# Attention and routed MoE on one core: logits and row transposes of two pairs of chunks together, other gating groups, constants beside chunk 0

## The chip, the cores and the metric

One core of one Trainium2 chip runs the whole program. The metric is the time of one execution on the device in microseconds, the median of several runs. TensorE is called PE here, VectorE DVE, ScalarE ACT, GpSimd POOL and SyncE SP; SP issues most DMAs.

## The reference, cut to what matters

Four batches of 768 tokens, eight heads of 64 dimensions. A decayed linear attention gives `x` of 3072 tokens by 512 features; a gate picks one of eight experts for each token, and that expert's two matrices (512 to 1024 to 512) are applied.

```python
for t in range(S):
    state = gamma * state + einsum('bhd,bhe->bhde', k[:, :, t], v[:, :, t])
    y[:, :, t] = scale * einsum('bhd,bhde->bhe', q[:, :, t], state)
x = y.transpose(0, 2, 1, 3).reshape(B * S, H * D)
logits = x @ w_gate
expert_idx = argmax(logits, axis=1)
gate_w = softmax(logits)[arange(N), expert_idx]
out[mask_e] = gate_w * (relu(x[mask_e] @ w1[e]) @ w2[e])      # for each expert e
```

All in float32; large products of the experts are split into a high and a low part.

## The kernel before, in words

The tokens are cut into 24 chunks of 128 (`C`), six to a batch (`CPB`). Twelve periods (`for n in range(last + 1)`, L545) each finish a pair of chunks, a = 2n and b = 2n + 1. The order in each engine's queue is written out by hand (`manual_schedule`): what stands first in the code stands first on its engine, and each engine works its queue in that order.

In a period PE does, in this order: `carry(n)` (the state's part of both outputs, L281), then the visit to the pair before: `logits(n - 1)` (L347), `rows` twice (transposes of `xT` into rows, L316) and `finish_logits` (transposes of the logits back to tokens, L356); then `update(b)` (L264, not at a batch's last chunk), `output(a)` and `output(b)` (L298), the `rank` products of a group where one is chosen (L408), `update(a + 2)`, and the scores of the next two chunks (L251). Four banks of PSUM, tags s0 to s3, hold the scores of two chunks, and between them the row transposes (s0 and s1).

ACT copies logits to `LT` (L353), transposed rows to `xrow` (L324), the state to `ub` (L275) and expert 0's weights to their high part (L139). DVE masks the scores (`Sb`, L260), evicts the outputs to `xT` (L312), reduces logits and does the gating. POOL scales v (`scale`, L238), makes the decay powers (`grow`), cuts low parts of weights (L140), and sends rows: `scatter_rows` (L758) writes one chunk's 128 rows of x to DRAM at the places that `KEY` names, by an indirect DMA.

Gating goes by groups of chunks, `GROUPS` (L44, first chunk and count): a group is chosen in the period after its last pair (`chosen`, L541): argmax, ranks within the expert, places, weights, and the label beside each row. Then its rows may be sent. Which chunks are sent where stands in three tables: `BEHIND` (L46, at the end of period n, behind the eviction of its second chunk), `AMID` (L47, behind the copy `LT` of period n) and `AFTER` (L48, behind the state's copy of `update(a + 2)`). Each entry has two chunks, and a small POOL copy to `gated` (L331) ahead of them waits for the named tile. Chunks 16 and 17 are sent in period 9 (`soon`, L590) as soon as they are labelled, and the first 320 rows of expert 0 are then fetched (`fetch_early`), turned in period 11 (`turn_early`) and used by the first expert's products, which fill PE's queue from there on (`early_pieces`, L801, first bank s2).

`xrow` holds a batch's six chunks, in two buffers. Chunks come by `load` (L223) on SP's queue, halves first: q and k turned (part 0), v and k as they are (part 1). `SPLITS` (L55) says in which period pieces of expert 0's weights are cut, `fetches` (L540) when the third quarter of them is fetched. Before the first chunk PE runs `WARM` products of ones (L506). Constants `cst` come in two DMAs, one on ACT's queue (L494) and one on SP's (L501).

The steps of the period that the change touches, as they stand in the loop:

```python
if n in AMID:
    send_behind(state["LT"][:, 0:1], AMID[n])
rows(a - 2, "s0")
rows(a - 1, "s1")
finish_logits(n - 1)
...
if n in BEHIND:
    send_behind(xTs[n][:, 0, C:C + 1], BEHIND[n])
...
    update(a + 2)
if n in AFTER:
    send_behind(ubs[(a + 2) % 3][:, 0, 0:1], AFTER[n])
...
    scale(a + 4)
```

Behind period 11 come the last pair's logits and rows, groups 4 and 5, the tail of the first expert's products and then the loop over the other experts.

Of the kernel before, what the change touches and what calls it, by code (L numbers as in the profile page):

```python
# [9 lines left out]
F32 = mybir.dt.float32  # L10
# [28 lines left out]
SLICE = P + 2  # L39
ROW = 4 * SLICE  # L40
MAXB = CMAX32 // 32
WARM = 10
FILL = (1, 3, 4)
GROUPS = ((0, 6), (6, 6), (12, 4), (16, 2), (18, 4), (22, 2))  # L44
FULL = 18
BEHIND = {3: (0, 1), 4: (4, 5), 6: (6, 7), 7: (10, 11), 8: (12, 13)}  # L46
AMID = {4: (2, 3), 7: (8, 9)}  # L47
AFTER = {8: (14, 15)}  # L48
AHEAD = 4
FIRST = AHEAD + 11  # L50
MID = (19, 20)
LATER = {6: (15, 16), 7: (17,), 8: (18,), 9: (19,), 10: (20,)}
_PIECES = {2: 3, 3: 2, 5: 3, 6: 1, 7: 3}
_ORDER = iter([(part, i) for part in range(4) for i in range(4)])
SPLITS = {n: tuple(next(_ORDER) for _ in range(c)) for n, c in _PIECES.items()}  # L55
BIG = 1 << 20
# [9 lines left out]
NCONST = _n  # L66
NFIRST = OFF["iota"][0]
NLOAD = OFF["ahead"][0]


def _constants():
# [30 lines left out]
def retention_moe(ctx, tc, qkv, w1, w2, cst, out):  # L102
# [102 lines left out]
    with ExitStack() as actx:  # L205
# [32 lines left out]
        def scale(g, engine=nc.gpsimd):  # L238
            c = g % CPB
            vs = wk.tile([P, H, D], F32, name="vs", bufs=3)  # L240
            engine.tensor_tensor(
                out=vs, in0=qs[g][:, 2].rearrange("a (h d) -> a h d", d=D),
                in1=cv[:, c, :].unsqueeze(2).broadcast_to([P, H, D]), op=ALU.mult)
# [63 lines left out]
        def evict(g):  # L307
            Y, c = Ys[g // 2], g % CPB
            if g % 2 == 0:
                xTs[g // 2] = wk.tile([P, NP, TW], F32, name="xT")  # L310
            xT = xTs[g // 2][:, :, (g % 2) * C:(g % 2 + 1) * C]
            nc.vector.tensor_tensor(out=xT.rearrange("a (r m) t -> a r m t", m=2), op=ALU.mult,  # L312
                                    in0=Y[:, :, 2 * (g % 2) * C:2 * (g % 2 + 1) * C].rearrange("a r (m t) -> a r m t", m=2),
                                    in1=G[:, c].rearrange("a (r m) t -> a r m t", m=2))

        def rows(g, tag, ps=ps_s):  # L316
# [7 lines left out]
            nc.scalar.copy(out=xrows[b][:, c, :, 0:P].rearrange("t q (k r) -> t q k r", r=32),  # L324
                           in_=tr.rearrange("t k (q r) -> t q k r", r=32))

        gated = gsm.tile([P, 1], F32, name="gated")
# [5 lines left out]
                send_rows(g)  # L333

        def send_rows(g):
            b, c = divmod(g, CPB)
            sent = scatter_rows(tc, x_rows, KEY[:, g, 0:1], xrows[b][:, c].rearrange("t q m -> t (q m)"), "sorted")

        def pad_rows(which, count, first):
            nc.vector.tensor_scalar(out=pads[:, which], in0=count, scalar1=k_("pos")[:, 0:1], scalar2=first,  # L340
# [4 lines left out]
            return scatter_rows(tc, x_rows, pads[:, i:i + 1], cs[:, 0:ROW], "sorted")  # L345

        def logits(t):  # L347
            L = bank(0, "L", (P, TW)) if t == NCH // 2 - 1 else ps_1.tile([P, TW], F32, name="L", tag="misc")
            for p in range(NP):
                nc.tensor.matmul(out=L[32 * p:32 * p + 32, :], lhsT=wgs[:, p, :], rhs=xTs[t][:, p, :],  # L350
                                 start=True, stop=True)
            LT = wk.tile([P, TW], F32, name="LT", bufs=1)
            nc.scalar.copy(out=LT, in_=L)  # L353
            state["LT"] = LT

        def finish_logits(t):  # L356
            i = [n for n, (a, w) in enumerate(GROUPS) if a <= 2 * t < a + w][0]
            a, w = GROUPS[i]
            both = ps_1.tile([P, 2, TW], F32, name="lp", tag="misc")
            lp, state["spare"] = both[:, 0].rearrange("p (c n e) -> p c n e", c=2, n=NP), both[:, 1]  # L360
            for ci in range(2):
                nc.tensor.transpose(out=lp[:, ci].rearrange("t p e -> t (p e)"),
                                    in_=state["LT"][:, ci * C:(ci + 1) * C], identity=ident)
            if w == 2:
                lgs[i] = state["spare"][:, 3 * w * E:4 * w * E].rearrange("p (i e) -> p i e", e=E)
            elif 2 * t == a:
                lgs[i] = gsm.tile([P, w, E], F32, name=f"lg{w}")
            nc.vector.tensor_reduce(out=lgs[i][:, 2 * t - a:2 * t - a + 2, :], axis=AX.X, op=ALU.add,
                                    in_=lp[:, :, :, 0:E].rearrange("t c p e -> t c e p"))


        exs = gsm.tile([P, CPB, E + 1], F32, name="exs")
# [1 line left out]
        def gating(i):  # L374
# [10 lines left out]

            def choose():

                lg, eq, pr = [state["spare"][:, n * w * E:(n + 1) * w * E].rearrange("p (i e) -> p i e", e=E)
                              for n in range(3)]
                mx, ed = v["mx"], v["ed"] = sm("mx"), sm("ed")  # L390
                nc.vector.tensor_reduce(out=mx, in_=lgs[i], axis=AX.X, op=ALU.max)  # L391
                if w == 2:
# [46 lines left out]
                nc.vector.reciprocal(out=gw, in_=gw)  # L439

            def label():
                b, c = divmod(a, CPB)
                x = xrows[b][:, c:c + w]
# [101 lines left out]
        for n in range(last + 1):  # L545
# [8 lines left out]
            if n > 0:  # L554
                if n == last:
                    turn_early()
                if n != soon:
                    logits(n - 1)
                if n == last:
                    for j, w, _ in first["pieces"]:  # L560
                        cut_high(nc, first["x"][0], first["xt"], j, w)
                if n in AMID:
                    send_behind(state["LT"][:, 0:1], AMID[n])
                rows(a - 2, "s0")
                rows(a - 1, "s1")
                finish_logits(n - 1)
            if n == 7:
                for i in SPLITS[n]:
# [653 lines left out]
```

## Time and profile before

| | |
|---|---|
| median of 3 runs | 413.22 us (411.82 to 414.07) |
| profiled execution, its own time | 408.67 us |
| its span, first to last instruction | 406.8 us |
| PE busy | 391.1 us (96%) |
| DVE, ACT, POOL busy | 239.9, 140.4, 181.5 us |
| mean granted clock of PE | 0.994 |
| DMA | 81.57 MB, 201 GB/s over the span |

The profiled execution is one run; its span leaves out what lies around the first and the last instruction. In a line of a timeline the first number is the start in us from the span's beginning, the second how long the merged instructions took together; in brackets stands how long the engine was idle ahead of it and what ended that.

### The profile page before, as it was taken

To read this page: it belongs to the slowest core of one execution; us is meant where nothing else is said; L and a number is where in the kernel's file an instruction comes from. 1 tells how busy PE (TensorE), PEld (TensorE's weight loads), DVE (VectorE), ACT (ScalarE), POOL (GpSimd) and SP (SyncE) were. 2 spreads that over 40 slices of the span, in tenths; PEclk is the share of its full clock that TensorE was granted. 3 is DMA by queue.
4 is the path that set the end of the run, shared out by engine and by line. 5 is a ranking of instruction groups with operands and counts; after the bars stand their busy time and mean duration, and the time that the engine had idled before them with its cause. 6 is when DMAs were issued, how large, how long until landed. Compare 5 with 4: busy or idle time off the path is not lost. (4 is left out here: it accounts for less than half of the span.)

```text
span 406.8 us, 8297 instructions
## 1 busy us (share of the span) xinstructions
PE 391.1 (96%) x3273; PEld 360.8 (89%) x3273; DVE 239.9 (59%) x468; ACT 140.4 (35%) x247; POOL 181.5 (45%) x176
## 2 busy tenths in 40 slices
PE   8999899889988999999999999999999999999985
PEld 5887787768888989999999999999999999999864
DVE  3467457756653478583847475667737748656111
ACT  1233244222521455531533343244334325424000
POOL 3647856562170507400374067028407714832722
PEclk9999999999999999999999999999999999999989
DMA  8999999937047939655543746284655546610101
GB/s 286 415 406 408 414 417 411 382 151 198 1 183 158 357 106 231 247 205 109 205 148 124 188 160 234 46 232 166 178 143 189 195 97 216 196 70 15 52 33 46
DMA packets 42328, 81.57 MB, mean 201 GB/s; under 512 B 4458, under 2 KB 18158, under 8 KB 39856
## 3 DMA queue, kind: packets, MB, share of 16 engines
q1 hardware_dynamic: 36768, 67.44, 49.5%
q0 software_dynamic: 5376, 13.49, 8.9%
q8 instruction: 26, 0.43, 0.4%
q10 hardware_dynamic: 144, 0.09, 0.2%
q14 instruction: 14, 0.11, 0.1%
HBM read 65.93 MB, written 15.68 MB: 201 GB/s over the span
## 5 line engine op out<-in xcount | busy, mean ns | idle before, releaser
L759 POOL DMA_INDIRECT out<-Z,sidx x90 | 102.8, 1142 | 142.5 <-DVE Z L940 117.2
L140 DVE TENSOR_TENSOR wlo<-raw,whi 128x1024 fp32r<-128x1024 f32 (+1 forms) x61 | 69.8, 1154 | 14.9 <-ACT whi L139 9.3
L139 ACT CAST whi<-raw 128x1024 fp32r<-128x1024 f32 (+1 forms) x72 | 67.1, 950 | 6.2 <-DMA raw<-w 6.1
L1083 PE MATMUL py<-hh,whi 128*128 128x452 f32 (+5 forms) x192 | 67.0, 349 | 0.0
L1083 PE MATMUL py<-hl,whi 128*128 128x452 f32 (+5 forms) x192 | 67.0, 349 | 0.0
L1083 PE MATMUL py<-hh,wlo 128*128 128x452 f32 (+5 forms) x192 | 66.8, 348 | 0.0
L1060 ACT ACTIVATE hh<-ph 128x452 fp32r<-128x452 f32 (+6 forms) x56 | 28.2, 506 | 88.6 <-PE ph L1055 71.2
L1061 DVE SCALAR_TENSOR_TENSOR hl<-ph,hh 128x452 fp32r<-128x452 f32 (+6 forms) x56 | 32.0, 574 | 39.3 <-ACT hh L1060 34.6
L1055 PE MATMUL ph<-xh,wlo 128*128 128x452 f32 (+6 forms) x224 | 50.1, 345 | 0.0
L1055 PE MATMUL ph<-xh,whi 128*128 128x452 f32 (+6 forms) x224 | 50.1, 345 | 0.0
L1055 PE MATMUL ph<-xl,whi 128*128 128x452 f32 (+6 forms) x224 | 50.0, 345 | 0.0
L1055 PEld LDWEIGHTS ph<-xh,whi 128*128 128x128 f32 x224 | 40.8, 188 | 0.9
L1055 PEld LDWEIGHTS ph<-xh,wlo 128*128 128x128 f32 x224 | 40.7, 188 | 0.8
L1055 PEld LDWEIGHTS ph<-xl,whi 128*128 128x128 f32 x224 | 40.7, 188 | 0.7
L1083 PEld LDWEIGHTS py<-hl,whi 128*128 128x128 f32 x192 | 36.0, 188 | 1.1 <-issue 0.3
L1083 PEld LDWEIGHTS py<-hh,whi 128*128 128x128 f32 x192 | 36.0, 188 | 1.0 <-ACT hh L1060 0.3
L1083 PEld LDWEIGHTS py<-hh,wlo 128*128 128x128 f32 x192 | 36.1, 188 | 0.7
L759 POOL DMA_INDIRECT x_sorted<-xrow,KEY x24 | 25.2, 1049 | 18.2 <-DVE mx L391 8.1
L781 ACT CAST xh<-buf 128x512 fp32r<-128x512 f32 (+7 forms) x26 | 14.3, 556 | 54.4 <-DVE buf L774 45.2
L260 DVE TENSOR_TENSOR Sb<-sp,cs 128x512 f32<-128x512 f32 x48 | 29.9, 682 | 4.4 <-PE sp L257 4.4
L935 DVE STREAM_TRANSPOSE Z<-py 128x416 f32<-128x416 f32 (+3 forms) x24 | 15.0, 625 | 21.3 <-PE py L1083 18.2
L304 PE MATMUL Y<-Sb,vs 128*64 128x128 f32 x384 | 24.6, 275 | 1.4 <-issue 1.4
(173 smaller groups left out, 535.7 us busy)
## 6 DMA issues: line engine op xcount, KB each, us to landing
raw<-w SPq DMA_DIRECT2D x32, 1024.0 KB
qkv_w<-qkv SPq DMA_DIRECT2D x12, 1024.0 KB
qkv_t<-qkv SPq DMA_DIRECT2D x7, 1024.0 KB
qkv_t<-qkv SPq DMA_DIRECT2D x8, 512.0 KB
buf<-x_sorted SPq DMA_DIRECT2D x12, 211.2 KB
x_sorted<-cs SPq DMA_DIRECT2D x6, 260.0 KB
buf<-x_sorted SPq DMA_DIRECT2D x8, 195.0 KB
out<-Z,sidx POOLq DMA_INDIRECT x90
```

The costliest lines, as they stand in the source:

```text
L139: nc.scalar.copy(out=hi[:, h], in_=raw[:, h])
L140: engine.tensor_tensor(out=lo[:, h], in0=raw[:, h], in1=hi[:, h].bitcast(F32), op=ALU.subtract)
L260: nc.vector.tensor_tensor(out=Sb[:, r], in0=sps[r], in1=causal.unsqueeze(1).broadcast_to([P, NP, C]), op=ALU.mult)
L304: nc.tensor.matmul(out=at(Y, g, half[o], r, m), lhsT=vp[:, p, half[r]], rhs=Sb[:, r, p, :], start=False, stop=True, skip_group_check=True)
L759: sc = tc.nc.gpsimd.indirect_dma_start(out=dst, out_offset=bass.IndirectOffsetOnAxis(ap=index, axis=0), in_=rows, in_offset=None, bounds_c ...
L781: nc.scalar.copy(out=xh[:, :, c0:c0 + w], in_=xt[:, :, t0:t0 + w])
L935: nc.vector.transpose(out=Zs[e][:, 0:nb, k, :], in_=py[:, 0:32 * nb].rearrange("p (j c) -> p j c", c=32))
L1055: nc.tensor.matmul(out=ph[:, :cap], lhsT=wparts[e, f // 4][a][:, kd, fo:fo + P], rhs=x[:, kd, :cap], start=(n == 0), stop=(n == 3 * KD - 1))
L1060: nc.scalar.activation(out=hh[:, :cap], in_=ph[:, :cap], func=AF.Relu)
L1061: nc.vector.scalar_tensor_tensor(out=hl[:, :cap], in0=ph[:, :cap], scalar=0.0, in1=hh[:, :cap].bitcast(F32), op0=ALU.max, op1=ALU.subtract)
L1083: nc.tensor.matmul(out=py[:, :cap], lhsT=a[:, f % 4, k * P:(k + 1) * P], rhs=x[:, :cap], **se)
```

## The change

Logits and row transposes are no longer done pair by pair. `SETS` joins pairs 1 and 2, 3 and 4, 5 and 6, 9 and 10; for these, `logits`, `rows` (four chunks, in all four banks s0 to s3) and `finish_logits` are done in the period behind the second pair, and the period behind the first pair has none. The copy `LT` and the transposed logits become twice as wide, `xT` gets a third buffer. The groups become 6, 4, 6, 2, 4, 2 chunks instead of 6, 6, 4, 2, 4, 2, so they are chosen in periods 3, 5, 8, 9 and 11 instead of 3, 6, 8, 9 and 11. Rows lie by group, in one buffer of six chunks and one of four that take turns. `BEHIND`, `AMID` and `AFTER` are filled anew. The constants become part of two transfers on SP's queue that also carry chunk 0's v and k (`head`, which takes the place of `xrow1` at the start); two ACT copies bring the constants to `cs`. Warm products are 8 instead of 10; a copy of the logits is left out for groups of four; one split and one fetch move.

```diff
-WARM = 10
+WARM = 8
-GROUPS = ((0, 6), (6, 6), (12, 4), (16, 2), (18, 4), (22, 2))
+GROUPS = ((0, 6), (6, 4), (10, 6), (16, 2), (18, 4), (22, 2))
+SETS = ((0,), (1, 2), (3, 4), (5, 6), (7,), (8,), (9, 10), (11,))
+PLACE = {t: (s, i) for s, pairs in enumerate(SETS) for i, t in enumerate(pairs)}
-BEHIND = {3: (0, 1), 4: (4, 5), 6: (6, 7), 7: (10, 11), 8: (12, 13)}
-AMID = {4: (2, 3), 7: (8, 9)}
-AFTER = {8: (14, 15)}
+BEHIND = {3: (0, 1), 4: (4, 5), 6: (6, 7), 7: (8, 9), 8: (10, 11)}
+AMID = {9: (14, 15)}
+AFTER = {3: (2, 3), 8: (12, 13)}
-_PIECES = {2: 3, 3: 2, 5: 3, 6: 1, 7: 3}
+_PIECES = {2: 3, 4: 2, 5: 3, 6: 1, 7: 3}
...
+            v, powers = (qs[g][:, 2], cv[:, c, :]) if g else (head[:, 0:DM], head[:, DM:DM + H])
...
-            kn = qs[g][:, 3]
+            kn = qs[g][:, 3] if g else head[:, HEAD:HEAD + DM]
...
-                xTs[g // 2] = wk.tile([P, NP, TW], F32, name="xT")
+                xTs[g // 2] = wk.tile([P, NP, TW], F32, name="xT", bufs=3)
...
-            b, c = divmod(g, CPB)
+            i, c = group_of(g)
             if c == 0:
-                xrows[b] = wk.tile([P, CPB, 4, SLICE], F32, name="xrow")
+                xrows[i] = wk.tile([P, (6, 4)[i % 2], 4, SLICE], F32, name=f"xrow{i % 2}", bufs=1)
...
         def logits(t):
+            k, i = PLACE[t]
+            if i < len(SETS[k]) - 1:
+                return
...
+            for i, pair in enumerate(SETS[k]):
+                for p in range(NP):
+                    nc.tensor.matmul(out=L[32 * p:32 * p + 32, i, :], lhsT=wgs[:, p, :], rhs=xTs[pair][:, p, :],
+                                     start=True, stop=True)
+            LT = wk.tile([P, 2, TW], F32, name="LT", bufs=1)
+            nc.scalar.copy(out=LT[:, 0:w], in_=L[:, 0:w])
...
+        def ready(t):
+            pairs = SETS[PLACE[t][0]]
+            return [2 * pair + i for pair in pairs for i in range(2)] if t == pairs[-1] else []
...
-                if w == 2:
-                    lg = lgs[i]
-                else:
+                if w == 6:
                     nc.vector.tensor_reduce(out=lg, in_=lgs[i].unsqueeze(3), axis=AX.X, op=ALU.add)
...
+        head = wk.tile([P, 2 * DM + NLOAD], F32, name="head", tag="xrow1", bufs=1)
         load(0, halves[0])
-        nc.scalar.dma_start(out=cs[:, 0:NFIRST], in_=cst[:, 0:NFIRST])
-        load(0, halves[1])
+        for part in (slice(0, HEAD), slice(HEAD, HEAD + DM + NLOAD - NFIRST)):
+            nc.sync.dma_start(out=head[:, part], in_=cst[:, part])
...
-        nc.sync.dma_start(out=cs[:, NFIRST:NLOAD], in_=cst[:, NFIRST:])
...
+        nc.scalar.copy(out=cs[:, 0:NFIRST], in_=head[:, DM:HEAD])
+        nc.scalar.copy(out=cs[:, NFIRST:NLOAD], in_=head[:, HEAD + DM:])
...
-        fetches = {6: 2}
+        fetches = {8: 2}
...
-                rows(a - 2, "s0")
-                rows(a - 1, "s1")
+                for i, g in enumerate(ready(n - 1)):
+                    rows(g, f"s{i}")
```

`finish_logits` gets the same test as `logits` and transposes two or four blocks at once.

## Rows read from the trace of the kernel before

**Rows 1.** The page, parts 1 and 5: busy time; groups with idle before them.
```profile
PE 391.1 (96%) x3273; PEld 360.8 (89%) x3273; DVE 239.9 (59%) x468; ACT 140.4 (35%) x247; POOL 181.5 (45%) x176
...
L304 PE MATMUL Y<-Sb,vs 128*64 128x128 f32 x384 | 24.6, 275 | 1.4 <-issue 1.4
```

**Rows 2.** The waits, all engines: total us, times, longest us.
```profile
ACT LT L353 <- PE tr L323: 8.6, 3, 4.0
...
PE lp L362 <- ACT LT L353: 3.0, 3, 1.1
```

**Rows 3.** PE's timeline, 0 to 26 us.
```profile
1.08 4.45 PE L506 MATMUL warm<-ones 128*128 128x512 bf16 x10 [1.08 <-DVE ones L162]
5.46 1.58 PE L257 MATMUL sp<-qkv_t 64*128 64x128 f32 x16
...
7.81 1.16 PE L257 MATMUL sp<-qkv_t 64*128 64x128 f32 x16
...
19.94 0.69 PE L272 MATMUL U<-vs,qkv_w 128*64 128x64 f32 x16
...
23.79 0.64 PE L350 MATMUL L<-xT,wgs 128*32 128x256 f32 x8
...
25.60 1.97 PE L304 MATMUL Y<-Sb,vs 128*64 128x128 f32 x32
```

**Rows 4.** The timeline of PE's weight loads, in period 6.
```profile
56.17 0.16 PEld L350 LDWEIGHTS L<-xT,wgs 128*32 128x32 f32 x8 [0.17 <-issue]
```

**Rows 5.** PE's timeline, 37 to 51 us, periods 4 and 5.
```profile
37.59 1.10 PE L291 MATMUL Y<-qkv_w,ub 64*64 64x128 f32 x32
...
39.19 1.09 PE L323 MATMUL tr<-cs,xT 128*128 128x128 f32 x8
41.22 0.44 PE L362 MATMUL lp<-cs,LT 128*128 128x128 f32 x2 [0.93 <-ACT LT L353]
...
43.84 0.64 PE L272 MATMUL U<-vs,qkv_w 128*64 128x64 f32 x16
...
46.40 1.89 PE L291 MATMUL Y<-qkv_w,ub 64*64 64x128 f32 x32
...
50.05 1.03 PE L323 MATMUL tr<-cs,xT 128*128 128x128 f32 x8
```

**Rows 6.** POOL's timeline, 18 to 94 us.
```profile
18.85 1.04 POOL L241 TENSOR_TENSOR vs<-qkv_w,cs 128x512 f32<-128x512 f32 x1 [0.67 <-DMA qkv_w<-qkv]
...
37.77 1.16 POOL L759 DMA_INDIRECT x_sorted<-xrow,KEY  x1 [0.75 <-ACT ub L275]
39.23 0.99 POOL L759 DMA_INDIRECT x_sorted<-xrow,KEY  x1 [0.30 <-issue]
40.22 1.07 POOL L241 TENSOR_TENSOR vs<-qkv_w,cs 128x512 f32<-128x512 f32 x1
...
73.90 0.98 POOL L759 DMA_INDIRECT x_sorted<-xrow,KEY  x1 [0.31 <-issue]
...
81.29 1.02 POOL L759 DMA_INDIRECT x_sorted<-xrow,KEY  x1 [0.63 <-ACT ub L275]
...
85.22 0.97 POOL L759 DMA_INDIRECT x_sorted<-xrow,KEY  x1 [0.31 <-issue]
...
91.35 2.05 POOL L241 TENSOR_TENSOR vs<-qkv_t,cs 128x512 f32<-128x512 f32 x2
```

**Rows 7.** PE's timeline, 76 to 105 us.
```profile
76.10 0.44 PE L362 MATMUL lp<-cs,LT 128*128 128x128 f32 x2 [1.09 <-ACT LT L353]
...
87.07 0.45 PE L304 MATMUL Y<-Sb,vs 128*64 128x128 f32 x4 [0.43 <-issue]
...
94.57 0.69 PE L272 MATMUL U<-vs,qkv_t 128*64 128x64 f32 x16
...
99.38 1.10 PE L291 MATMUL Y<-qkv_t,ub 64*64 64x128 f32 x32
...
104.13 0.85 PE L814 MATMUL ph<-xh,whi 128*128 128x320 f32 x4
```

More of the change, by code (lines that the diff above doesn't have):

```diff
@@ L68 @@
 NLOAD = OFF["ahead"][0]
+HEAD = DM + NFIRST
 def _constants():
@@ L240, in scale @@
             vs = wk.tile([P, H, D], F32, name="vs", bufs=3)
+            v, powers = (qs[g][:, 2], cv[:, c, :]) if g else (head[:, 0:DM], head[:, DM:DM + H])
             engine.tensor_tensor(
-                out=vs, in0=qs[g][:, 2].rearrange("a (h d) -> a h d", d=D),
-                in1=cv[:, c, :].unsqueeze(2).broadcast_to([P, H, D]), op=ALU.mult)
+                out=vs, in0=v.rearrange("a (h d) -> a h d", d=D),
+                in1=powers.unsqueeze(2).broadcast_to([P, H, D]), op=ALU.mult)
             vss[g] = vs.rearrange("a (n t) d -> a n (t d)", t=2)
@@ L314, in evict, with group_of @@
                                     in1=G[:, c].rearrange("a (r m) t -> a r m t", m=2))
+        def group_of(g):
+            return [(i, g - a) for i, (a, w) in enumerate(GROUPS) if a <= g < a + w][0]
         def rows(g, tag, ps=ps_s):
-            b, c = divmod(g, CPB)
+            i, c = group_of(g)
             if c == 0:
-                xrows[b] = wk.tile([P, CPB, 4, SLICE], F32, name="xrow")
+                xrows[i] = wk.tile([P, (6, 4)[i % 2], 4, SLICE], F32, name=f"xrow{i % 2}", bufs=1)
             tr = ps.tile([P, NP, P], F32, name="tr", tag=tag)
@@ L323, in rows @@
                 nc.tensor.transpose(out=tr[:, p, :], in_=xTs[g // 2][:, p, (g % 2) * C:(g % 2 + 1) * C], identity=ident)
-            nc.scalar.copy(out=xrows[b][:, c, :, 0:P].rearrange("t q (k r) -> t q k r", r=32),
+            nc.scalar.copy(out=xrows[i][:, c, :, 0:P].rearrange("t q (k r) -> t q k r", r=32),
                            in_=tr.rearrange("t k (q r) -> t q k r", r=32))
@@ L335, in send_rows @@
         def send_rows(g):
-            b, c = divmod(g, CPB)
-            sent = scatter_rows(tc, x_rows, KEY[:, g, 0:1], xrows[b][:, c].rearrange("t q m -> t (q m)"), "sorted")
+            i, c = group_of(g)
+            sent = scatter_rows(tc, x_rows, KEY[:, g, 0:1], xrows[i][:, c].rearrange("t q m -> t (q m)"), "sorted")
         def pad_rows(which, count, first):
@@ L347, in logits @@
         def logits(t):
[L348 to L354, printed above, removed]
-        def finish_logits(t):
-            i = [n for n, (a, w) in enumerate(GROUPS) if a <= 2 * t < a + w][0]
-            a, w = GROUPS[i]
[L359 to L363, printed above, removed]
-            if w == 2:
-                lgs[i] = state["spare"][:, 3 * w * E:4 * w * E].rearrange("p (i e) -> p i e", e=E)
-            elif 2 * t == a:
+            k, i = PLACE[t]
@@ new lines, in logits @@
+            if i < len(SETS[k]) - 1:
+                return
+            L = bank(0, "L", (P, 2, TW)) if t == NCH // 2 - 1 else ps_1.tile([P, 2, TW], F32, name="L", tag="misc")
+            w = i + 1
+            for i, pair in enumerate(SETS[k]):
[3 more added lines that the diff above has]
+            LT = wk.tile([P, 2, TW], F32, name="LT", bufs=1)
@@ new lines, in logits @@
+            nc.scalar.copy(out=LT[:, 0:w], in_=L[:, 0:w])
+            state["LT"] = LT.rearrange("p i t -> p (i t)")
+        def ready(t):
+            pairs = SETS[PLACE[t][0]]
+            return [2 * pair + i for pair in pairs for i in range(2)] if t == pairs[-1] else []
+        def finish_logits(t):
+            k, i = PLACE[t]
+            if i < len(SETS[k]) - 1:
+                return
+            n = 2 * len(SETS[k])
+            first_, i = 2 * SETS[k][0], group_of(2 * t)[0]
+            a, w = GROUPS[i]
+            lp = ps_1.tile([P, 4, C], F32, name="lp", tag="misc")
+            for ci in range(n):
+                nc.tensor.transpose(out=lp[:, ci], in_=state["LT"][:, ci * C:(ci + 1) * C], identity=ident)
+            state["spare"] = spare = lp.rearrange("t c (n e) -> t (c n) e", n=NP)
+            if w == n:
+                lgs[i] = spare[:, 0:w, E:2 * E]
+            elif first_ == a:
@@ L367, in finish_logits @@
                 lgs[i] = gsm.tile([P, w, E], F32, name=f"lg{w}")
-            nc.vector.tensor_reduce(out=lgs[i][:, 2 * t - a:2 * t - a + 2, :], axis=AX.X, op=ALU.add,
-                                    in_=lp[:, :, :, 0:E].rearrange("t c p e -> t c e p"))
+            nc.vector.tensor_reduce(out=lgs[i][:, first_ - a:first_ - a + n, :], axis=AX.X, op=ALU.add,
+                                    in_=lp[:, 0:n].rearrange("t c (n e) -> t c e n", n=NP)[:, :, 0:E, :])
         exs = gsm.tile([P, CPB, E + 1], F32, name="exs")
@@ L386, in choose @@
             def choose():
-                lg, eq, pr = [state["spare"][:, n * w * E:(n + 1) * w * E].rearrange("p (i e) -> p i e", e=E)
-                              for n in range(3)]
+                lg, eq, pr = [state["spare"][:, 0:w, n * E:(n + 1) * E] for n in range(1, 4)]
                 mx, ed = v["mx"], v["ed"] = sm("mx"), sm("ed")
                 nc.vector.tensor_reduce(out=mx, in_=lgs[i], axis=AX.X, op=ALU.max)
-                if w == 2:
-                    lg = lgs[i]
-                else:
+                if w == 6:
                     nc.vector.tensor_reduce(out=lg, in_=lgs[i].unsqueeze(3), axis=AX.X, op=ALU.add)
@@ L441, in label @@
             def label():
-                b, c = divmod(a, CPB)
-                x = xrows[b][:, c:c + w]
+                x = xrows[i][:, 0:w]
                 nc.scalar.copy(out=x[:, :, :, P + 1], in_=gw.broadcast_to([P, w, 4]))
@@ L1208 @@
     a, b = OFF["gates"]
-    cst = np.concatenate([cst[:, :a], gates, cst[:, b:]], axis=1)
+    cst = np.concatenate([natural(v)[0, 0], cst[:, :a], gates, natural(k)[0, 0], cst[:, b:]], axis=1)
     arrays = {
```

## The prediction

> **What bounds the kernel now.** I read the page first. TensorE (PE) is busy for 391.1 of the 406.8 us [rows 1], so a change pays only where PE has gaps, or where it makes gaps. The whole change lies in the attention part, before the first expert block, whose first hidden product starts at 104.13 us [rows 7]; behind that the order of the work stays as it was. The total is therefore that start, moved by what the change gains or loses ahead of it. Then I read PE's timeline with its bracketed gaps, then the waits, then GpSimd's (POOL's) timeline beside it.
>
> The reader is to see three things. First, a "visit" (logits, row transposes, logit transposes) takes 1.81 us of PE in each period: from 23.79 to 25.60 [rows 3]. Second, PE stands in front of the logit transposes for 3.0 us in three places, waiting for ScalarE's copy `LT`, and that copy in turn starts late by PE's own word: it waits 8.6 us in three places for PE, although PE's logits are long issued [rows 2]. The gaps are 0.93 at 41.22 [rows 5] and 1.09 at 76.10 [rows 7], and a third like the first in period 7. Third, in each of these places POOL is at a pair of indirect scatters: 37.77 to 40.22 and until 74.88 [rows 6]. The gap ends 1.0 to 1.2 us behind the pair's last scatter (40.22 to 41.22, 74.88 to 76.10): what PE has finished seems to reach the others only when the pair is over. Another such pair lies on period 5, where carry and logits take 3.65 us (46.40 to 50.05) and the same two take 1.60 in period 4 (37.59 to 39.19) [rows 5]: 2.05 lost. A fourth place is the output of period 9, whose matmuls have 1.4 us of "issue" gaps, the only ones of that line in the whole span [rows 1], while POOL issues the second pair of a run of four scatters (81.29 to 86.19) [rows 6].
>
> **The change part by part** (minus is a gain; places by period n).
>
> *a. Start.* Chunk 0's v and k now arrive with the constants in two transfers on SP's queue, in place of one more on ScalarE's queue and one later on SP's; the bytes are the same. PE starts scores at 5.46 [rows 3]. What is won here is soon capped: the update at 19.94 follows chunk 4's scaled v, which POOL finishes at 18.85 + 1.04 = 19.89 after a wait for that chunk's load [rows 3, 6], and as many bytes lie ahead of that load as before. Two ScalarE copies of constants are new; ScalarE is idle there, and if they came late POOL's decay powers would, ahead of the same cap. Bounds -0.4 and +0.2; I take -0.1, near the cap. Two of ten warm matmuls go, 0.43 each (4.45 for ten) [rows 3]; they end as the scores begin, so this frees nothing while the load is what scores wait for: 0, with the clock as a rival below.
>
> *b. Merged visits.* Pairs 1+2, 3+4, 5+6 and 9+10 go together in periods 3, 5, 7 and 11; periods 2, 4, 6 and 10 lose their visit. The matmuls stay as many. What goes is the opening and closing of four visits; the weight load ahead of the logits idles 0.17 in one [rows 4], so 0 to -0.35 each with the other two changes of form. I take -0.2 each, -0.8. The copy `LT` becomes twice as wide, but sixteen transposes stand in front of the logit transposes instead of eight. Four row copies in a row on ScalarE lie beside outputs and scores; were that cover gone, the next scores would wait for banks, some tenths each. Two DVE copies of logits go, hidden beside PE.
>
> *c. Gaps in front of the logit transposes* (4, 7, 8: 2.95). Period 4 has no visit now. In 7 the visit is twice as long, and its pair (6,7) is no longer gated behind a group's labels, since that group is chosen in period 5: it starts before the period. In 8 the pair (8,9) no longer comes behind another pair sent in period 7, so it starts and ends earlier against the visit. All gone is -2.95, only period 4's gone is -0.93; I take -2.6, a few tenths left in 8.
>
> *d. The 2.05 of period 5.* Chunks 4,5 now go out right after scale(10), so beside the scores that end period 4. Chunks 2,3 were there before, and from 43.84 to 46.40 update and scores followed each other without a gap [rows 5]. Bounds 0 and -2.05; I take -1.75.
>
> *e. A new wait in period 4.* Chunks 2,3 are sent in period 3 directly behind 0,1, ahead of scale(10) in POOL's queue. Before, scale(10) stood behind one pair, at 40.22, 1.07 long [rows 6], and the update that needs it started at 43.84 [rows 5]. A run of four took 4.90 (81.29 to 85.22 + 0.97) [rows 6]: from 37.77 to 42.67, or 42.85 with the longer first one, then 1.07: 43.74 to 43.92. PE is there at 43.84 - 1.81 (no visit) - 0.93 (no gap) = 41.10. It waits 2.6 to 2.8. With every scatter as long as 37.77's 1.16 it would be 3.5. Behind this update stand scores and the next carry; DVE's evictions and copies use the time. I take +2.7 (2.6 to 3.5).
>
> *f. Eight scatters in period 9.* 10,11 take the place of 12,13 at its start and 12,13 that of 14,15; then 14,15 follow at once, and 16,17 behind the labels as before. So a third pair joins the run, and lies on PE's output, ranks and updates. Nearest row: the second pair, 1.4 [rows 1]. It costs from 0 (the first pair of that run, no gap) to the 2.45 of a whole pair (37.77 to 40.22) [rows 6] and some 0.5 behind it: 2.9. I take +1.4. Scaled v of chunk 21 comes after 16,17 on POOL: before it was ready at 91.35 + 1.03 and needed at 94.57 [rows 6, 7], 2.2 spare; 1.81 of visit less ahead of it leaves 0.4. No wait, but little is left.
>
> *g. Rest.* `fetch(0, 2)` and one split move a period later and free the chunk loads behind them; expert 0's third piece is first cut in period 6: 0. `xrow0` and `xrow1` are single now; each is sent at least a period before it is written again: 0. Period 11 is longer by the visit of pair 9, as 10 is shorter; from 99.38 to 104.13 [rows 7] becomes some 6.3.
>
> Sum: -0.1 - 0.8 - 2.6 - 1.75 + 2.7 + 1.4 = -1.15. The profiled execution took 408.67 (span 406.8); that would be 407.5. The median of the runs is 413.22, 4.6 above it, and the difference carries over: **412.1**.
>
> The Trainium skill, "SBUF — State Buffer", section "SBUF: two separate sides", says that of the engines only VectorE and GpSimd share a port, and that PE waits for nobody there. By it scatters on POOL should cost PE nothing, and c, d and f would have to be laid to something else. The gaps of [rows 5 to 7] coincide with pairs, which the trace shows and the page doesn't explain; what follows if the page is right is the second rival.
>
> **The rivals.**
> *Faster, 410.3 (chance 0.28).* The third pair in period 9 holds nothing up, as the first didn't, and c and d are won nearly whole: with f at 0 the sum is -2.55, with every other term at its better end -0.4 - 1.4 - 2.95 - 2.05 + 2.6 = -4.2; I take -2.9, near the first. For it: of the nine pairs before 95 us only five cost PE anything. Against: the late pairs of runs did.
> *Slower, 415.5 (0.12).* The gaps belong to the place, not to the pair: visits of 7 and 8 keep theirs, period 5 its stop. Then -0.1 - 0.8 - 0.93 + 2.7 + 1.4 = +2.3. It decides as soon as c and d together bring less than the 3.2 that update(10)'s wait and the third pair cost beyond a and b. For it: the wait in e is sure, being POOL's order, while the gains depend on where pairs fall. Against: gaps in exactly those periods that a pair opens.
> *The clock, 414.3 (0.07).* Warm matmuls run at the 1.2 GHz level (0.43 for 512 columns); 16 scores took 1.58 from 5.46 and 1.16 from 7.81 [rows 3], so the level rose in the first. PE now idles some 0.85 before the scores. If the rise had to be earned anew from 5.46, as it took from 1.08 to about 6.4, it would come about 4.4 later, and half of that is lost: +2.2, -1.15 + 2.2 = +1.1. The Trainium skill, "TensorE: Matmul & The Clock Gate", section "What's actually happening", says that the throttled level is the default and activity releases it, which speaks against fewer warm matmuls. The trace shows one rise and no fall here.
> *No change, 413.2 (0.08).* Period 11 needs the rows that POOL scatters last (16,17); if their fetch sets its start, what is won before is waited out there.
>
> **How the numbers follow.** The forecast has 0.45, with a range of its own of 411.0 to 413.4. About 0.5% (2.1 us) is what a measurement can tell from no change. Faster by more (under 411.1): 0.85 of the first rival and 0.15 of the forecast, 0.31. Slower (over 415.3): most of the second rival, some of the clock's, 0.15. Within: 0.54. For eight in ten the range goes from 409.4, deep into the faster case, to 415.2, into the slower one.
>
> **What would show it.** Right: no gap in front of the logit transposes of periods 7 and 8 over 0.4; PE stands 2.6 or more before the update of period 4, released by POOL's `vs`; the first hidden product starts at about 103.0. Wrong: that wait is missing or moves the carry behind it too; "issue" gaps of over 2.5 in period 9; gaps of about 1 remain in 5, 7 or 8; matmuls of the start at 1.2 GHz beyond 7 us.

## The result: 1.4% slower

The changed kernel takes 419.38 us (median of 6; 415.30 to 424.31, of which the longest, a slow execution, is left out of the ratio), the kernel before beside it 412.52 (median of 6; 409.57 to 414.07). The ratio is 1.014, interval 1.0095 to 1.0186: 5.8 us slower on 412.5 (interval 3.9 to 7.7). The forecast was 412.1, at most 415.2. The profiled execution of the changed kernel took 419.12 with a span of 417.3, that of before 408.67 with 406.8; as that one is faster than each of the six runs of before, 10.5 us between the two traces is more than the runs show.

The two traces are set side by side at points where PE has done the same work, so at carries ahead of which no visit is outstanding (only the rank products of the second group, 0.24 us, move from period 6 to period 5):

| PE reaches | before | after | later by | lost in between |
|---|---|---|---|---|
| carry of period 4 | 37.59 | 37.83 | 0.24 | 0.24 |
| carry of period 6 | 55.58 | 57.26 | 1.68 | 1.44 |
| carry of period 8 | 72.32 | 73.11 | 0.79 | -0.89 |
| logits at the head of period 9 | 81.23 | 81.81 | 0.58 | -0.21 |
| carry of period 10 | 91.19 | 96.24 | 5.05 | 4.47 |
| first hidden product | 104.13 | 108.36 | 4.23 | -0.82 |
| first product of the late rows | 138.38 | 144.09 | 5.71 | 1.48 |
| end of the span | 406.81 | 417.29 | 10.48 | 4.77 |

The page after, its lines of PE's busy time and of the outputs, which answer to [rows 1]: 2.6 us more of busy time, and 3.3 us of "issue" in front of the outputs instead of 1.4.

```profile
PE 393.7 (94%) x3271; PEld 364.5 (87%) x3271; DVE 239.7 (57%) x462; ACT 139.5 (33%) x245; POOL 181.2 (43%) x176
...
L308 PE MATMUL Y<-Sb,vs 128*64 128x128 f32 x384 | 26.9, 282 | 3.3 <-issue 3.3
```

Period 9 is where most of the time ahead of the hidden product went. PE's timeline after, periods 4 to 9 (start, length, engine and line, tile, count; in brackets the idle time in front and what ended it):

```profile
40.06 0.49 PE L308 MATMUL Y<-Sb,vs 128*64 128x128 f32 x5 [0.35 <-issue]
...
43.85 0.65 PE L308 MATMUL Y<-Sb,vs 128*64 128x128 f32 x6 [0.16 <-issue]
44.44 0.69 PE L276 MATMUL U<-vs,qkv_w 128*64 128x64 f32 x16
...
48.07 2.09 PE L363 MATMUL L<-xT,wgs 128*32 128x256 f32 x16
...
70.51 0.69 PE L276 MATMUL U<-vs,qkv_t 128*64 128x64 f32 x16 [0.69 <-issue]
...
76.62 0.44 PE L383 MATMUL lp<-cs,LT 128*128 128x128 f32 x2 [0.82 <-ACT LT L366]
...
87.69 0.49 PE L308 MATMUL Y<-Sb,vs 128*64 128x128 f32 x5 [0.97 <-issue]
89.15 0.17 PE L428 MATMUL pf<-EA,us 128*128 128x16 bf16 x1 [0.97 <-issue]
...
90.59 0.21 PE L433 MATMUL pf<-EA,ones 128*128 128x16 bf16 x2 [1.15 <-issue]
90.72 1.97 PE L308 MATMUL Y<-Sb,vs 128*64 128x128 f32 x16
...
93.48 1.94 PE L261 MATMUL sp<-qkv_w 64*128 64x128 f32 x16
```

Then POOL's timeline after, in the same periods:

```profile
42.11 0.97 POOL L778 DMA_INDIRECT x_sorted<-xrow,KEY  x1 [0.30 <-issue]
43.11 1.05 POOL L245 TENSOR_TENSOR vs<-qkv_w,cs 128x512 f32<-128x512 f32 x1
...
81.95 1.02 POOL L778 DMA_INDIRECT x_sorted<-xrow,KEY  x1 [0.68 <-ACT ub L279]
...
88.49 0.97 POOL L778 DMA_INDIRECT x_sorted<-xrow,KEY  x1 [0.30 <-issue]
92.21 0.97 POOL L778 DMA_INDIRECT x_sorted<-xrow,KEY  x1 [2.75 <-ACT xrow L462]
93.48 0.97 POOL L778 DMA_INDIRECT x_sorted<-xrow,KEY  x1 [0.30 <-issue]
94.47 2.05 POOL L245 TENSOR_TENSOR vs<-qkv_t,cs 128x512 f32<-128x512 f32 x2
```

And stretches of periods 9 and 10 (length, busy time of each engine, then the granted clock, DMA share, GB/s):

```profile
81.00:88.00 7.00, 5.32 (x82) 3.87 (x80) 3.97 (x14) 2.04 (x6) 5.29 (x8) 1.00 0.57 222
88.00:95.10 7.10, 4.99 (x57) 4.75 (x55) 2.31 (x10) 1.17 (x5) 3.72 (x5) 0.52 0.32 124
```

Six scatters run from 81.95 to 89.46. From the third on PE gets few products at a time, with nothing to wait for that the trace shows ("issue"); the gaps in its output and rank products make 3.79 us (0.30, 0.40, 0.97, 0.97, 1.15), where the trace of before had 1.4 us of them in all [rows 1]. While they last the granted clock falls to half, from 88.3 to 95.1: 16 scores take 1.94 us, 1.16 at the 2.4 GHz level [rows 3]. The second output of period 9 starts here in the trace of before:

```profile
87.72 1.09 PE L304 MATMUL Y<-Sb,vs 128*64 128x128 f32 x16
```

With it the 4.47 us of period 9 fall into two parts. From the logits to this output it takes 8.91 us (81.81 to 90.72) instead of 6.49 (81.23 to 87.72), 2.42 more: the gaps. From there to the next carry it takes 5.52 (to 96.24) instead of 3.47 (to 91.19), 2.05 more: the clock.

In period 4 the same is seen in small: the 32 output products take some 5 us, in bursts, instead of 1.9, so that the update behind them starts at 44.44, later than with the visit in front of it (43.84 [rows 5]). The wait predicted there is not seen, because these gaps fill the same time: POOL's scaled value is ready at 44.16, PE arrives at 44.44.

### The profile page after: what moved, and what is told of

It reads as the page before. It is cut to its first block, busy times and chain, and to the rows that moved or that the text cites. A ratio compares the mean times of both kernels' runs of the same rounds, so it can differ in the third digit from the quotient of the medians.

```text
span 417.3 us, 8288 instructions
## 1 busy us (share of the span) xinstructions
PE 393.7 (94%) x3271; PEld 364.5 (87%) x3271; DVE 239.7 (57%) x462; ACT 139.5 (33%) x245; POOL 181.2 (43%) x176
## 5 line engine op out<-in xcount | busy, mean ns | idle before, releaser
L1074 PE MATMUL ph<-xh,wlo 128*128 128x452 f32 (+6 forms) x224 | 50.1, 345 | 0.0
L1074 PE MATMUL ph<-xh,whi 128*128 128x452 f32 (+6 forms) x224 | 50.1, 345 | 0.0
L778 POOL DMA_INDIRECT x_sorted<-xrow,KEY x24 | 24.2, 1007 | 18.7 <-DVE mx L411 9.2
L308 PE MATMUL Y<-Sb,vs 128*64 128x128 f32 x384 | 26.9, 282 | 3.3 <-issue 3.3
```

Source lines behind the costliest of these rows:

```text
L308: nc.tensor.matmul(out=at(Y, g, half[o], r, m), lhsT=vp[:, p, half[r]], rhs=Sb[:, r, p, :], start=False, stop=True, skip_group_check=True)
L778: sc = tc.nc.gpsimd.indirect_dma_start(out=dst, out_offset=bass.IndirectOffsetOnAxis(ap=index, axis=0), in_=rows, in_offset=None, bounds_c ...
L1074: nc.tensor.matmul(out=ph[:, :cap], lhsT=wparts[e, f // 4][a][:, kd, fo:fo + P], rhs=x[:, kd, :cap], start=(n == 0), stop=(n == 3 * KD - 1))
```

## Experiments

The runs fell on chips of two sorts. On three chips no "issue" gaps stand beside the scatters and the kernel before takes 393.0 to 393.3 us (on one of them at two times); on another it takes 407.0, with gaps as in the profile predicted from. Each ratio is to the kernel before on the same chip. Call the chips gapless and gapped.

### One part alone, or undone: e1 to e4 (gapless)

**e1**, the kernel before with the new sending table for rows 8 to 15, six in a run in period 9:
```
-BEHIND = {..., 7: (10, 11), 8: (12, 13)}; AMID = {4: (2, 3), 7: (8, 9)}; AFTER = {8: (14, 15)}
+BEHIND = {..., 7: (8, 9), 8: (10, 11)};   AMID = {4: (2, 3), 9: (14, 15)}; AFTER = {8: (12, 13)}
```


> The kernel before, with only its sending table changed to that of the changed kernel for rows 8 to 15: rows 8, 9 behind period 7, 10, 11 behind period 8, 12, 13 after its update, 14, 15 amid period 9, so that GpSimd sends six pairs of halves in one run while TensorE does period 9. Theory 1 (the run of six scatters in period 9 holds TensorE, which then falls to 1.2 GHz for some us): 3 to 5 us slower than before (415.5 to 417.5), a stretch of half clock within 85 to 97 us, and period 9 about 4 us longer than its 9.96 us. Theory 2 (the loss comes from the start, with the constants in chunk 0's rows and two warm-up products fewer) and theory 3 (it comes from the visits of two pairs together): within 1 us of before, no half clock there.

Measured: 1.0023 (1.0014 to 1.0032), 0.9 us; the clock full throughout its trace; one wait of 0.65 for POOL's `vs` in period 10. Theory 1 fails on this chip.

**e2**, the changed kernel with a run of four:
```
-AMID = {9: (14, 15)}           ... for g in range(FULL - 2, FULL):
+AMID = {}                      ... for g in range(FULL - 4, FULL):
```


> The changed kernel, with rows 14, 15 sent together with 16, 17 at the end of period 9, so that the run ahead of them is four and not six. Theory 1: 3 to 5 us faster than the changed kernel (414.5 to 416.5), no half clock within 85 to 97 us, period 9 about 10 to 11 us instead of 14.4; if sending 14 to 17 in one run delays the first fetch of the sorted rows it gives 1 to 2 us of that back. Theories 2 and 3: within 1 us of the changed kernel (418.5 to 420.5).

Measured: 1.0225 (1.0206 to 1.0245). No gain. But the edit makes no run of four here: the labels are there in time, and POOL sends all eight one behind the other (79.47 to 89.49), so theory 1 isn't tested by it.

**e3**, the changed kernel with the groups of before:
```
-GROUPS = ((0, 6), (6, 4), (10, 6), ...)   SETS = (..., (3, 4), (5, 6), (7,), ...)
+GROUPS = ((0, 6), (6, 6), (12, 4), ...)   SETS = (..., (3, 4), (5,), (6, 7), ...)
+BEHIND 7: (10, 11), 8: (12, 13); AMID {}; AFTER 3: (2, 3), 6: (8, 9), 8: (14, 15); xT in two buffers
```


> The changed kernel with the group sizes of before (6, 6, 4, 2, 4, 2); the visits of two pairs are then pairs 1+2, 3+4, 6+7 and 9+10, and no run of scatters in period 9 is longer than the four of the kernel before. Theory 1: 4 to 6 us faster than the changed kernel, that is within 1.5 us of the kernel before (411 to 414.5). Theory 3 (the visits of two pairs cost more than they save): stays 4 to 7 us slower than the kernel before. Theory 2 (start): also stays 4 to 7 us slower.

Measured: 1.0213 (1.0189 to 1.0237), with waits of PE for POOL's `vs` of 2.86 in period 4 and 2.96 in period 7.

**e4**, the changed kernel with the start of before (first constants on ScalarE's queue, the rest behind chunk 3, `WARM = 10`):

> The changed kernel with the start of before: the first constants on ScalarE's queue, the rest behind chunk 3, chunk 0 loaded in two parts, ten warm-up products. Theory 2: 4 to 6 us faster than the changed kernel (413 to 415). Theory 1: within 1 us of the changed kernel (418.5 to 420.5), since the 0.9 us that the changed kernel is late in period 1 is down to 0.24 us by period 4.

Measured: 1.0174 (1.0158 to 1.019). Theory 2 explains little. All of e2 to e4 have what e1 lacks, the visits of two pairs above all. Their traces show where: e4 stands 2.85 us in front of the update of chunk 10 in period 4 and 2.59 in front of that of chunk 21 in period 10, both released by POOL's `vs`.

### Before and after on a gapless chip: e10, e11

> The kernel before itself, for a trace of it from the chip of this call (the chips of the calls so far differ: on one the products of periods 3 to 10 ran without issue gaps beside the scatters, and the kernel before took 393 us; on the others with gaps of 0.2 to 1.1 us, and it took 407 to 413 us). On a chip without such gaps all theories expect no wait of TensorE over 0.7 us up to the first hidden product, which starts at 95 to 96.5 us; on one with gaps the first hidden product starts at 102 to 105 us.

> The changed kernel itself on the chip of this call. Theory 4 (TensorE waits for GpSimd's scaled values in periods 4 and 10, where the work that covered the wait has moved a period on): without issue gaps, waits of 2.5 to 3 us before the updates of both periods, ratio 1.017 to 1.023. With issue gaps, 3 to 5 us of them in periods 4 and 9 in their place, ratio 1.008 to 1.018.

e10: 0.9994 (0.9983 to 1.0004). e11: 1.0206 (1.0164 to 1.0249). Windows of e10 and then of e11 (columns as above), and of e11 the waits of PE up to the first hidden product (total, times, longest) and its timeline:

```profile
37.00:53.00 16.00, 15.98 (x302) 13.64 (x298) 10.34 (x20) 7.12 (x17) 12.79 (x15) 1.00 1.01 413
...
84.00:96.00 12.00, 12.00 (x214) 10.14 (x207) 6.91 (x14) 4.52 (x11) 3.88 (x4) 1.00 0.66 185
```
```profile
37.00:53.00 16.00, 13.13 (x238) 11.43 (x237) 10.93 (x19) 2.81 (x8) 12.06 (x14) 0.89 1.02 420
...
84.00:96.00 12.00, 9.39 (x191) 8.54 (x191) 6.24 (x22) 2.51 (x8) 9.24 (x12) 0.94 0.51 189
```
```profile
PE U L276 <- POOL vs L245: 5.5, 2, 2.9
```
```profile
46.21 0.74 PE L276 MATMUL U<-vs,qkv_w 128*64 128x64 f32 x16 [2.87 <-POOL vs L245]
46.88 3.58 PE L261 MATMUL sp<-qkv_w 64*128 64x128 f32 x32
...
93.59 0.69 PE L276 MATMUL U<-vs,qkv_t 128*64 128x64 f32 x16 [2.61 <-POOL vs L245]
94.11 3.26 PE L308 MATMUL Y<-Sb,vs 128*64 128x128 f32 x32
...
106.32 0.85 PE L833 MATMUL ph<-xh,whi 128*128 128x320 f32 x4
```

e10 is what the kernel before is where scatters hold nothing up: PE busy for 15.98 of 16.00 and 12.00 of 12.00 us, so no gap for the change to close; its first hidden product starts at 95.68. In e11 two waits appear, each followed by some us at the 1.2 GHz level (32 scores in 3.58 instead of 2.06, 32 outputs in 3.26 instead of 1.92). The first hidden product is 10.64 later, the end of the span 10.71: behind the attention part nothing differs. Of the 10.64, 2.41 are there by period 4 (0.7 from the start, see e14, the rest with a fall of the clock at 9.2 that e14 and e16 don't have), 4.70 come in periods 4 and 5, 4.04 in 10 and 11, and periods 6 to 9 give 0.5 back.

In period 9 e10's POOL sends six scatters ahead of the scaling of chunk 21, from 76.04, and scales at 83.52; e11's sends eight in one run, from 82.39, and scales at 92.47. And in e10 PE has the visit of pair 9 between the carry of period 10 and the update (84.31 to 86.13); in e11 it stands in period 11.

### Taking the waits away: e6, e7, e8 (gapped), e12 (gapless)

e5 is the changed kernel itself on the gapped chip.

> The changed kernel itself, beside the kernel before on the chip of this call, as the measure for the others of the call. All theories: ratio 1.010 to 1.022. Theory 4 (TensorE waits for GpSimd's scaled values: the update of chunk 10 in period 4 and that of chunk 21 in period 10 stand behind scatters in GpSimd's order, and the logits and transposes that used to cover the wait have moved to the next period): two waits of 2.5 to 3 us before update products, in periods 4 and 10, where TensorE isn't held by the scatters themselves; where it is held, the time is lost in issue gaps of the products in front of them.

Measured: 1.0124 (1.0069 to 1.0178).

**e6**, e7 and their sum e8 move a scaling ahead of scatters in POOL's order:
```
 update(a + 2)
+if n == 3: scale(a + 4)          # e6, chunk 10; left out further down
+if n == soon - 1: scale(b + 4)   # e7, chunk 21; left out in period 9
 if n in AFTER: send_behind(...)
```


> The changed kernel with the scaling of chunk 10 put ahead of the sending of rows 2, 3 in GpSimd's order of period 3, everything else as it is. Theory 4: the wait before the update in period 4 goes, 2.5 to 3 us faster than the changed kernel of this call; the wait of period 10 stays. Theory 1 (run of six scatters) and theory 2 (start): within 0.7 us of the changed kernel.

Measured: 1.0124 (1.0066 to 1.0182), no gain.

> The changed kernel with the scaling of chunk 21 put ahead of the sending of rows 12, 13 in period 8 (instead of behind that of rows 16, 17 in period 9). Theory 4: the wait before the first update of period 10 goes, and with it the stretch at half clock behind it: 2.5 to 4 us faster than the changed kernel of this call. Theories 1 and 2: within 0.7 us of it, or up to 1 us slower, since all scatters of period 9 start one scaling (1.05 us) later.

Measured: 1.0175 (1.0131 to 1.022), no gain, rather worse.

> Both scalings put ahead of the scatters, and the start of the kernel before (ten warm-up products, constants on ScalarE's queue). Theory 4: 6 to 8 us faster than the changed kernel of this call, that is from 1 us faster to 1 us slower than the kernel before; the visits of two pairs alone cost nothing. Theory 3 (the visits of two pairs cost more than they save): stays at least 4 us slower than the kernel before.

Measured: 1.0119 (1.0073 to 1.0166), 4.1 us above before by the medians: theory 4 fails here, theory 3 just holds. PE's timeline of e6, then of e8:

```profile
88.20 0.23 PE L430 MATMUL pf<-tot,ones 128*128 128x24 bf16 x3 [0.54 <-issue]
...
89.62 0.17 PE L433 MATMUL pf<-EA,ones 128*128 128x8 bf16 x1 [1.16 <-issue]
```
```profile
91.39 0.46 PE L294 MATMUL Y<-qkv_t,ub 64*64 64x128 f32 x4 [0.96 <-issue]
...
94.25 0.70 PE L294 MATMUL Y<-qkv_t,ub 64*64 64x128 f32 x3 [0.98 <-issue]
94.88 1.12 PE L275 MATMUL U<-vs,qkv_t 128*64 128x64 f32 x16
```
On the gapped chip nothing is won: the gaps go where the scatters go. Scattering later in e8 moves them from output and rank products to the carry.

**e12** is e8 again, on a gapless chip.

> The changed kernel with both scalings ahead of the scatters and the start of the kernel before. On a chip without issue gaps, theory 4: both waits gone, 0.997 to 1.006 of the kernel before; theory 3 (the visits of two pairs cost of themselves): 1.012 or more. On a chip with issue gaps both expect what the last call gave, 1.007 to 1.017, the gaps taking the place of the waits.

Measured: 1.0201 (1.0174 to 1.0228): theory 4, as put, fails; the figure is theory 3's, but e13 below shows that the visits alone don't make it. The waits of PE up to the hidden product, then those of ACT from 57 to 66 us:

```profile
PE U L275 <- POOL vs L244: 3.4, 2, 3.0
PE lp L382 <- ACT LT L365: 2.6, 1, 2.6
```
```profile
ACT whi L142 <- DMA raw<-w: 6.9, 1, 6.9
```
The wait of period 4 fell from 2.87 to 0.46, as meant. Two others took its place. In period 7 the logit transposes wait 2.62 for the copy `LT`, which stands on ACT behind a split of expert 0's third weight piece, and ACT has waited 6.9 us for that transfer: it is asked for later than before (`fetches`: at 48.95, in e10 at 42.36), and its split starts at 63.97 (in e10 it landed at 56.07). In period 10 the second update waits 2.95 for chunk 22's scaled value, behind the same eight scatters. In e11 the same split starts at 64.09, but PE, late by the wait of period 4, needs the copy only at 67.5: the first waits had covered these.

### What the merging itself costs: e9, e13 to e18 (gapless)

Theory 5 lays the loss to the placing of what PE needs, behind scatters or behind a late transfer; theory 6 to the missing single visits, which cover such lateness in any placing.

**e9**, the kernel before with the new POOL order of period 4: `AMID 4: (2, 3)` becomes `AFTER 3: (2, 3)`.

> The kernel before with rows 2, 3 sent at the end of period 3, ahead of the scaling of chunk 10 in GpSimd's order, as in the changed kernel, but with the visits of before: period 4 keeps its logits and transposes of one pair. Theory 4: on a chip without issue gaps, a wait before the update of chunk 10 of 0.7 to 1.3 us (the 2.85 us seen without the visit, less the 1.5 to 2.1 us that the visit takes), ratio 1.001 to 1.004: the visit covers the rest. With issue gaps, the gap of 0.93 us in front of the logit transposes of period 4 moves into the outputs or goes; within 0.5% of before. Theory 3: no wait at all.

Measured: 1.0019 (1.001 to 1.0028), a wait of 1.12 in front of the update of period 4, both as theory 4 said. So a visit in its place covers 1.75 of the 2.87.

**e15**, the changed kernel with single visits: `SETS = tuple((t,) for t in range(12))`.

> The changed kernel with one visit per pair, one period each, as before; its groups, sending table, weight pieces and start are kept. Theory 6: the waits before the updates of periods 4 and 10 fall from 2.9 and 2.6 us to 1.0 and 0.7 us or less (a visit takes 1.9 us), the kernel is 3 to 4.5 us faster than the changed one on a chip without issue gaps (1.009 to 1.013 of before). Theory 5: the same waits fall, but the visits then lie on the path of period 5 and 11 no longer, so it gains the same there; what tells them apart is merged_fixed. Rival (the four-bank visits themselves cost): 6 us or more faster than the changed kernel.

Measured: 1.0069 (1.0055 to 1.0082); again as e17: 1.0075 (1.0062 to 1.0089). Waits of PE in e15:

```profile
PE U L276 <- POOL vs L245: 2.1, 2, 1.3
```
The two waits are 1.28 and 0.80, a little more than foreseen, and the clock stays full. By the ratios e15 is 5.4 us faster than the changed kernel, more than theory 6's 3 to 4.5 and less than the 6 of its rival. So in the changed kernel's placing the merging costs 1.3%, two thirds of the loss.

**e13** keeps merged visits and repairs the placing: e3 with the start, weight pieces and third weight fetch of before, and
```
+if n in AFTER and n != soon - 1: scale(a + 4)     # chunks 10 and 16 ahead of the scatters
 if n in AFTER: send_behind(...)
```
**e14** is e13 with the start of the changed kernel.

> Visits of two pairs kept (pairs 1+2, 3+4, 6+7, 9+10), but the rest as before: group sizes 6, 6, 4, 2, 4, 2, six scatters and not eight in period 9, the start, the weight pieces and the third weight fetch of before; the scalings of chunks 10 and 16 ahead of the scatters of their periods. Theory 5 (the loss is the placing: what stands behind scatters or behind a late weight transfer; the visit of two pairs costs nothing of itself): 0.996 to 1.004 of the kernel before, no wait of TensorE over 1 us up to the first hidden product on a chip without issue gaps. Theory 6 (the single visit of each period is the cover for delays that are there in any placing): waits of 1 to 3 us in periods 4, 7 or 10 stay, 1.007 or more.

> The kernel merged_fixed with the start of the changed kernel (constants in chunk 0's rows, eight warm-up products). Theory 2: 0.5 to 1.5 us slower than merged_fixed, since the 0.6 to 1.0 us that it is late in period 1 has no wait left to hide in. If the start costs nothing: within 0.3 us.

Measured: e13 1.0036 (1.0024 to 1.0047), e14 1.0045 (1.0031 to 1.0059). Waits of PE in e13:

```profile
PE tr L329 <- DVE Sb L263: 0.6, 1, 0.6
PE U L275 <- POOL vs L244: 0.4, 2, 0.2
PE Y L294 <- DVE xT L315: 0.4, 1, 0.4
PE ph L832 <- ACT xrow L330: 0.3, 1, 0.3
```
Theory 5 comes out: 2% shrink to a sixth, with the visits still merged, and no wait is over 0.64. But it is not a win. At period 6 e13 stands level with e10 (+0.02); of the 1.82 at the first hidden product (97.50) 1.45 come in periods 7 and 8, where PE, with no visit in period 7, waits for DVE twice (0.39 and 0.64) and the sixteen transposes take 2.45 instead of 1.97. e14 is 0.7 us slower than e13 by the medians: its start is 0.69 late by period 4, and nothing takes that in; the two intervals overlap.

The last two, e16 (e2 again) and e18 (e1 again):

> The changed kernel with rows 14 to 17 sent together at the end of period 9. On a chip with issue gaps, theory 1: the gaps of period 9 fall by 2 us or more, 2 to 5 us faster than the changed kernel (1.000 to 1.008 of before). On a chip without them: as measured, 1.020 to 1.025 of before.

> The changed kernel with visits of one pair, its groups, sending table, weight pieces and start kept. On a chip with issue gaps: theory 1 (the run of six scatters in period 9) expects 1.008 to 1.018 of before, as the changed kernel; theory 6 (the cover that the single visits give) expects 0.998 to 1.006. On a chip without gaps both expect what was measured there, 1.005 to 1.009.

> The kernel before with the sending table of the changed kernel for rows 8 to 15, six scatters in a run in period 9. On a chip with issue gaps: theory 1 expects 3 to 5 us more than before (1.007 to 1.012), with gaps or half clock in period 9; theory 6 expects 0.997 to 1.003, the gaps of the pair taken out of period 7 coming back in period 9. On a chip without gaps: 1.001 to 1.004, as measured.

Measured: e16 1.0199 (1.0179 to 1.0219), e18 1.0017 (1.0008 to 1.0026), both gapless again. What the run of six, and single visits, would do on a gapped chip was therefore not settled; there the cause rests on the two traces and on e6 to e8, where the gaps moved with the scatters. No version was faster than the kernel before.

## Why the prediction was wrong

The sum was -1.15; between the two traces the table gives +4.23 at the first hidden product, the point to which the sum was made. Of the 5.4 between them step f has 3.1, and periods 4 and 5 have 1.4. Two of the prediction's own signs of being wrong are there: the wait in period 4 is missing, and period 9 has more than 2.5 of issue gaps. By its steps:

- **a, start (-0.1).** +0.24 by period 4 here, with one merged visit in it; e14 less e13, where nothing covers it, has period 4 0.69 later. The sign was wrong: all constants now lie ahead of chunk 1 on SP's queue, and the second scores (8.78) wait 1.1 us for it.
- **b, merged visits (-0.8).** A merged visit takes 3.34 us (28.67 to 32.01 in e13) against twice 1.81: 0.28 less, a little more than the 0.2 taken. The time isn't kept: e13, with two merged visits behind it, is level with e10 at period 6.
- **c, gaps in front of the logit transposes (-2.6).** Those of periods 4 and 7 are gone, 0.93 each; period 8's stayed, 0.82 where [rows 7] had 1.09. About -2.1, and period 7 gave 0.69 of it back in a gap ahead of its second update.
- **d, the 2.05 of period 5 (-1.75).** Half won: the carry runs free, but the pair 4,5 still falls on the logits, 16 of which take 2.09, while 16 take 1.07 in period 7. About 1.0 is lost instead of 2.05.
- **e, the wait in period 4 (+2.7).** Right in place and size: 2.85 to 2.87 on gapless chips. On the predicted chip it shows as bursts of products: the update starts at 44.44, 3.3 later than the output (from 39.39) at its usual pace would let it, within the bounds. Periods 4 and 5 together: predicted +2.7 less 0.93 and 1.75, measured +1.44.
- **f, eight scatters in period 9 (+1.4, at most 2.9). This step failed.** It measured 4.47. The gaps, 2.42 more than before, lie within its bounds, though it took less: it priced the third pair by the second, but the gaps grew along the run (0.3 and 0.4, then about 1 each), up to the rank products. What lies outside is the fall of the clock, 2.05, which step f put at nothing; the trace of before had shown no fall behind its shorter gaps.
- **f, chunk 21's scaled value.** The prediction reckoned only with the visit that left period 10 ("2.2 spare; 1.81 of visit less ahead of it leaves 0.4") and left out the two more scatters in front on POOL, 1.28 each by their starts: -2.2, not +0.4. On the gapless chips this is the wait of 2.61. On the predicted chip it cost nothing: PE was so late that POOL stood 2.75 us for the labels behind the six scatters, and the value, ready at 95.5, was needed at 97.27.

The rivals were none of them it: the "slower" one laid the gaps to the place, but two of the four went, and half of period 5's; the clock's was about the start, while the fall came in period 9. Yet the clock's rival is real: of the eleven traces with the new start three (e5, e7, e11) run the first carry at the pace of 1.2 GHz (16 products in 1.13 us instead of 0.67) and reach the carry of period 4 at 39.8 to 40.6 us, the others at 37.8 to 38.5; of the nine with the old start none does.

Behind the hidden product, where the prediction expected no difference since no instruction's order is changed, the two traces part by another 6.3: 1.5 by the late rows, of which a stretch at 1.2 GHz from 129.3 to 132.7 is a part. Of the 4.8 behind them 4.1 are waits of PE in the experts: 4.0 instead of 1.9 for ACT's `hh`, and 1.3 for DVE's `Z` and 0.7 of issue gaps that the trace of before lacks. On the gapless chip there is nothing of the kind (10.64 and 10.71). Whether that belongs to the change is open; the ratio's 5.8 us say that part of it does not.

Two things underneath. First, c and d rested on gaps that the kernel before has on one sort of chip: e10 has none, so there the change could win at most a and b. The prediction took them for the kernel's own. Second, moving a visit was priced as moving PE time from one period to the next, with no loss. e9 and e15 show on gapless chips what a visit did where it stood: it covered 1.6 to 1.8 us of POOL's lateness (2.87 to 1.12 or 1.28, 2.61 to 0.80). Merged, it leaves every other period without that cover. e13 shows the other half: where the operands come early, the merged visits cost little.

## What to carry to other kernels

Before moving work off a period, list for that period every operand that PE will need next and when its engine delivers it, counting all that is queued ahead on that engine after the change; work that stands in front of a late operand is free, and its removal buys a wait. Taking away one wait in a chain like this shows the next, so undo a whole part (here the merging) before mending waits one by one. And compare the kernel before on two chips, if there are two, before building on gaps that have no cause in the program.

## What the hardware showed

- **Scatters and PE.** On the chip of the prediction's profile and on that of e5 to e8 PE got its products in bursts of one to six, mostly 0.7 to 0.8 us apart (40.06, 40.82, 41.58), in places 1.4, while indirect scatters ran; on three others it ran through. e10, the same program, has no wait from period 1's outputs to the first hidden product. The Trainium skill, "SBUF — State Buffer", section "SBUF: two separate sides", has PE wait for nobody at SBUF's ports. The gapless chips agree; on the gapped ones PE stood (0.97 and 1.15 in period 9), and no run shows whether at SBUF or elsewhere. The cause is open: the traces show nothing that PE waits for, and in the trace after, from 84 to 92 us, the DMA queues carry the scatters' packets alone, so a load of instructions doesn't show there either.
- **The clock.** It fell to 1.2 GHz after PE had stood for 2.6 to 2.9 us (e11: 46.7 to 50.1, 94.5 to 97.9), among the gaps of period 9 (88.3 to 95.1), and in e11 at 9.2, after waits of 0.48 and 1.18 for loads. It did not always: of the twelve waits of 2.5 to 3.0 us in e2, e3, e4, e11, e12 and e16 nine brought a fall and three did not, and e2 and e16, one program with the same wait of 2.87 in period 4, differ in it (mean clock of 37 to 53 us: 1.00 and 0.89). The waits of up to 1.28 in e15 brought none. The Trainium skill, "TensorE: Matmul & The Clock Gate", section "What's actually happening", takes the throttled level for the default, which activity lifts; the falls behind waits agree. In e11 each such wait cost itself and then about 1.5 us more (3.58 less 2.06).
